# The multiply of the softmax bias moved from VectorE to ScalarE for 70 of 72 groups of an attention and soft-MoE kernel

## The chip, the cores and the metric

One Trainium2 chip, one core. The time is device microseconds of one execution; the kernel before took 293.11 us (median of 3 runs, 291.14 to 293.45). The profiled execution took 293.25 us, of which 291.5 us lie between its first and its last instruction. Engine names as in the profile: PE is TensorE, PEld its weight loads, DVE is VectorE, ACT is ScalarE, POOL is GpSimd, SP issues the transfers.

## The reference, cut to what matters

Windowed attention with a distance bias, then a soft mixture of experts over its output. The change touches the softmax of the attention alone.

```python
scores = scale * np.matmul(q, k.transpose(0, 1, 3, 2))          # (8, 8, 576, 576), scale = 1/8
mask = (rel >= 0) & (rel < window)                                # window = 128
scores = np.where(mask, scores + bias[None], -1000000000.0)
scores = scores - np.max(scores, axis=-1, keepdims=True)
attn = np.exp(scores)
attn = attn / (np.sum(attn, axis=-1, keepdims=True) + 1e-09)
attn_out = np.matmul(attn, v)
# then: logits = x @ phi; softmax over tokens and over slots; experts relu(. @ w1) @ w2; combine
```

## The kernel before, in words

Batches are 8, and a batch's 576 queries are cut into four tiles of 128 and one of 64. The unit of work is a **group**: one query tile and four of the eight heads (for the tile of 64, all eight heads), so 9 groups in a batch and 72 in all. One loop (L780 to L807) runs over the groups `i`, and in each turn it works on several groups at once, as a pipeline: the front of the softmax of group `i`, the transposes of group `i-3` (`FLAG = 3`), the product with the values of group `i-4` (`LAG = 4`), and the scores of group `i+1`. Each engine keeps the order in which the code writes its instructions (`tc.manual_schedule`), and waits at the head of its own queue.

For group `i` a turn does this:

- `softmax_front(i, i-1)` (L314): on DVE `merge` (L267, L269, L271) puts the masked halves of the 128x512 scores together in PSUM, `rowmax` (L289) takes the negated maximum of each of four heads, `inverse` (L301) takes 1/sum of group `i-1`, `bias` (L292) multiplies the negated maximum of group `i` by 1/8 into the tile `nb`, and `normalise` (L306) multiplies the four 128x128 tiles of group `i-1` by their 1/sum. `total` (L297) of group `i-1`, a copy of the four sums, runs on POOL between the exponentials that give the sums and `inverse`.
- `flip(i-3)` (L351) transposes the normalised tiles on PE into the one PSUM tile `pt`; `split(i-3)` copies it out on ACT (L358), and two masked selects on POOL (L360 and L362; L365 and L367 for the tile of 64) cut it into two triangles. The first tile of a batch needs none of the two selects.
- `run("act", i)`: on ACT `x_keep` (L417) of an earlier tile, and in five turns of a batch a small step of the token softmax (L444, L475, L479, L502, L537).
- `values(i-4)` (L387) on PE, and every second group `x_store` (L403) on ACT.
- `scores(i+1)` (L235 and L240, or L247 and L254) on PE, into the one of two PSUM tiles `s4` that group `i-1` has left.
- `expo(i)` (L341) on ACT: four exponentials of 128x128 with `nb` as their bias and with the row sums as a second output, each followed by a read of the accumulator.
- the DVE's parts of the token softmax and of the slot sums (L451 to L455, L486, L522, L533, L534) and, a piece at a time inside `softmax_front`, L543 to L546.

The call of `bias` stands in `softmax_front`, which is written ahead of `split`, `run("act", i)`, `x_store` and `expo` of the same turn. `number[key]` is a group's place from 0 to 71; `EAGER` is 2. After the loop (from about 222 us on) come the rest of the last batch, the experts and the combination; nothing there calls `bias`.

Of the kernel before, what the change touches and what calls it, by code (L numbers as in the profile page):

```python
# [28 lines left out]
SCALE = 0.125  # L29
# [13 lines left out]
EAGER = 2  # L43
# [24 lines left out]
def tile_attn_softmoe(  # L68
# [13 lines left out]
    nc = tc.nc  # L82
# [56 lines left out]
    st = {}  # L139
# [12 lines left out]
    number = {key: i for i, key in enumerate(groups)}  # L152
# [136 lines left out]
        nc.vector.tensor_reduce(st[key]["mx"][:, us], merged(key, us), axis=AX.X, op=ALU.max, negate=True)  # L289

    def bias(key, us):
        nc.vector.tensor_scalar_mul(st[key]["nb"][:, us], st[key]["mx"][:, us], SCALE)  # L292

    def total(key, us, eng=None):
        if "rs" not in st[key]:
# [18 lines left out]
    def softmax_front(new, old):  # L314
        first, eager = number[old] == 0, 0 < number[old] < EAGER
        merge(new)
        filler()
        if not eager:
            total(old, ALL, nc.gpsimd)
        if first:  # L320
            inverse(old, ALL)
            normalise(old, LO, nc.scalar.mul)
        rowmax(new, ALL)
        filler()
        if not first and not eager:
            inverse(old, ALL)
        filler()
        bias(new, ALL)
        if eager:
            total(old, ALL)  # L330
            inverse(old, ALL)
        filler()
        normalise(old, HI if first else ALL)
# [443 lines left out]
    with tc.manual_schedule(engines=ORDERED):  # L777
        scores(0)
        loads(0)
        for i in range(n):  # L780
            new = groups[i]
            run("pre", i)
            if i:
                softmax_front(new, groups[i - 1])
            else:
                for us in (LO, HI):
                    merge(new, us)
                    rowmax(new, us)
                    bias(new, us)
                    expo(new, us)  # L790
            if i >= FLAG:
                flip(groups[i - FLAG])
                split(groups[i - FLAG])
            run("act", i)
            if i >= LAG:
                values(groups[i - LAG])
                after_values(i, groups[i - LAG])
            if i + 1 < n:
                scores(i + 1)
            if i + 1 < n - 1:  # L800
                loads(i + 1)
            run("mid", i)
            if i:
                expo(new)
            run("pe", i)
            load_weights_at(i)
            run("dve", i)  # L807
# [307 lines left out]
```

## Time and profile before

| what | value |
|---|---|
| median of 3 runs | 293.11 us (291.14 to 293.45) |
| profiled execution | 293.25 us, span 291.5 us, mean granted TensorE clock 0.979 |
| PE, DVE, ACT, POOL busy | 273.9, 240.9, 206.9, 93.0 us |
| the loop over groups | first `bias` of group 1 at 9.8 us, last of group 71 at 221.9 us |
| `bias` L292 | 73 instructions: 71 of 128x4 at 156 ns, 2 of 128x2 at 169 ns |
| exponentials L341 | 288, 374 ns each, and 288 reads of 211 ns |
| copies on ACT: L358, L403, L417 | 599, 564 and 610 ns each |
| `normalise` L306 on DVE | 286, 339 ns each |
| `rowmax` L289, `merge` L269 on DVE | 698 and 686 ns each |

A row of the timeline gives start, duration, engine, line, operation, tiles, count and, in brackets, how long the engine sat idle before it and who released it. Two instructions of one engine can overlap: the next one starts before the one ahead of it has ended, so what a row costs its engine is the distance to the next start.

### The profile page before, as it was taken

The page shows a single profiled execution, that of the slowest core. Times are in us where ns is not written, and L with a number is a line of the kernel's source. Part 1 is how long each engine was busy: PE and PEld are TensorE (multiplying, and loading weights), DVE is VectorE, ACT ScalarE, POOL GpSimd, SP SyncE. Part 2 cuts the span into 40 slices and gives each one's busy share as a digit, 9 for nine tenths or more (in the row PEclk, how much of TensorE's full clock was granted, in tenths as well). Part 3 has the DMA queues.
Part 4 walks back from the last instruction along what each step waited for, and adds up shares of the span by engine and source line. Part 5 has one row for each costly group of instructions (what it writes and reads, how often), then busy time and mean ns, then how long its engine had stood idle before and what let it go on. Part 6 is the DMA issues. An engine that isn't in the chain of part 4 may idle for free.

```text
span 291.5 us, 13052 instructions
## 1 busy us (share of the span) xinstructions
PE 273.9 (94%) x5131; PEld 194.9 (67%) x5131; DVE 240.9 (83%) x746; ACT 206.9 (71%) x810; POOL 93.0 (32%) x207
## 2 busy tenths in 40 slices
PE   8499999999999999999998999999899999999990
PEld 4267777777677777776776777667677753587660
DVE  3899999999989999988999999979889455646442
ACT  2798888978988988987897887978687331035460
POOL 2025515442443344244414540644465002000000
PEclk9689999999999999999999999999999999999996
DMA  6544378877686887867686878776547779998897
GB/s 197 207 138 137 106 216 270 271 225 256 209 272 206 277 260 254 259 217 255 202 274 217 282 215 283 228 237 193 168 148 265 256 243 342 416 418 335 327 390 290
DMA packets 36753, 72.58 MB, mean 249 GB/s; under 512 B 4402, under 2 KB 15316, under 8 KB 36692
## 3 DMA queue, kind: packets, MB, share of 16 engines
q1 hardware_dynamic: 35972, 71.24, 73.4%
q8 instruction: 40, 0.66, 0.9%
q10 hardware_dynamic: 720, 0.51, 0.6%
q14 instruction: 21, 0.17, 0.2%
HBM read 62.29 MB, written 9.44 MB: 246 GB/s over the span
## 4 chain that ended last, share of the span: by engine, by line
PE 52%; DVE 38%; issue 3%; ACT 3%; POOL 2%; DVEq 0%; ACTq 0%; POOLq 0%
DVE area L306 13%; PE xp L387 10%; DVE s L289 9%; PE op L960 5%; PE s L254 5%; PE pt L351 5%; DVE s L269 5%; PE hp L924 5%; PE po L984 3%; DVE s L267 3%; PE xq L408 3%; PE s L247 2%; ACT area L341 2%; PE lp L426 2%; PE ap L509 2%
## 5 line engine op out<-in xcount | busy, mean ns | idle before, releaser
L341 ACT ACTIVATE area<-s,nb 128x128 f32<-128x128 f32 x288 | 102.5, 374 | 21.0 <-DVE nb L292 19.9
L306 DVE TENSOR_SCALAR area<-area,rs 128x128 f32<-128x128 f32 x286 | 79.4, 339 | 0.6 <-DVE nb L292 0.3
L387 PE MATMUL xp<-area 128*64 128x128 f32 (+1 forms) x1104 | 75.4, 271 | 3.5 <-POOL area L360 1.4
L387 PEld LDWEIGHTS xp<-area 128*64 128x64 f32 x1104 | 56.2, 136 | 18.9 <-issue 9.8
L341 ACT ACTIVATION_READ_ACCUMULATOR area<-s,nb 128x1 f32 x288 | 60.8, 211 | 0.0
L289 DVE TENSOR_REDUCE s<-s 128x4 f32<-128x512 f32 x71 | 49.5, 698 | 2.2
L358 ACT COPY area<-pt 128x512 f32<-128x512 f32 x70 | 41.9, 599 | 12.3 <-PE pt L351 12.0
L351 PE MATMUL pt<-unit_r,area 128*128 128x128 f32 x284 | 46.0, 285 | 0.0
L297 POOL TENSOR_SCALAR rs<-sm 128x4 f32<-128x4 f32 x70 | 13.7, 196 | 100.1 <-ACT area L341 99.2
L254 PE MATMUL s<-kq 64*32 64x160 f32 x1792 | 42.0, 302 | 0.0
L351 PEld LDWEIGHTS pt<-unit_r,area 128*128 128x128 f32 x284 | 32.2, 143 | 14.3 <-PE s L254 5.0
L360 POOL TENSOR_SCALAR_AFFINE_SELECT area<-area 128x512 f32<-128x512 f32 x48 | 31.5, 656 | 27.0 <-ACT area L358 25.9
L269 DVE COPY_PREDICATED s<-cst,s 128x512 f32<-128x512 int32 x48 | 32.9, 686 | 0.9 <-PE s L254 0.9
L362 POOL TENSOR_SCALAR_AFFINE_SELECT area<-area 128x512 f32<-128x512 f32 x48 | 31.4, 654 | 3.3
L254 PEld LDWEIGHTS s<-kq 64*32 64x32 f32 x1792 | 29.6, 108 | 0.6
L247 PE MATMUL s<-ramp,ones 64*32 64x320 bf16 x448 | 18.8, 311 | 4.8 <-ACT area L341 4.4
L403 ACT COPY area<-xp 128x512 f32<-128x512 f32 (+1 forms) x37 | 20.9, 564 | 2.2 <-PE xp L387 1.9
L408 PE MATMUL xq<-unit_r,area 128*128 128x128 f32 x136 | 22.0, 284 | 0.4
L417 ACT COPY area<-xq 128x512 f32<-128x512 f32 x34 | 20.7, 610 | 0.0
L408 PEld LDWEIGHTS xq<-unit_r,area 128*128 128x128 f32 x136 | 14.5, 141 | 6.1 <-issue 3.2
L986 ACT COPY ob<-po 128x512 f32<-128x512 f32 x19 | 10.4, 591 | 11.4 <-PE po L984 11.2
L986 DVE COPY ob<-po 128x512 f32<-128x512 f32 x17 | 11.2, 687 | 6.6 <-PE po L984 5.8
(171 smaller groups left out, 327.4 us busy)
## 6 DMA issues: line engine op xcount, KB each, us to landing
w<-w SPq DMA_DIRECT2D x53, 512.0 KB, 5.2
out<-ob SPq DMA_DIRECT2D x36, 256.0 KB, 3.2
kq<-q_t SPq DMA_DIRECT2D x69, 128.0 KB, 3.1
kq<-k_t SPq DMA_DIRECT2D x32, 256.0 KB, 4.0
area<-v_n SPq DMA_DIRECT2D x31, 256.0 KB, 4.3
area<-w SPq DMA_DIRECT2D x8, 512.0 KB, 3.9
area<-v_n SPq DMA_DIRECT2D x12, 128.0 KB, 3.2
kq<-w SPq DMA_DIRECT2D x3, 512.0 KB, 6.0
```

Source lines behind the costliest of these rows:

```text
L247: nc.tensor.matmul(s4[32 * c:32 * c + 32, 2 * par:2 * par + 2, 32 * r:32 * r + WIN], lhsT=ones[rows, 0:32], rhs=ramp[rows, h], start=True, ...
L254: nc.tensor.matmul(s4[32 * c:32 * c + 32, 2 * par + jj, 32 * r:32 * r + WIN], lhsT=qt[rows, 2 * h + jj if t == 4 else jj, 32 * r:32 * r + 32],
L269: nc.vector.copy_predicated(s4[:, :, P:2 * P], bc(mask_u, 1, 4), s4[:, :, 0:P])
L289: nc.vector.tensor_reduce(st[key]["mx"][:, us], merged(key, us), axis=AX.X, op=ALU.max, negate=True)
L306: mul(p4[:, u], p4[:, u], st[key]["rs"][:, u:u + 1])
L341: nc.scalar.activation(s["p4"][:, u], merged(key, u), AF.Exp, bias=s["nb"][:, u:u + 1], scale=SCALE, accum_out=s["sm"][:, u:u + 1],)
L351: nc.tensor.transpose(s["pt"][:, u], s["p4"][:, u], ident)
L358: copy(pa[:, us], s["pt"][:, us])
L360: nc.gpsimd.affine_select(pp[:, us], pa[:, us], [[0, m], [-1, P]], ALU.is_gt, 0.0, base=0, channel_multiplier=1)
L362: nc.gpsimd.affine_select(pa[:, us], pa[:, us], [[0, m], [1, P]], ALU.is_ge, 0.0, base=0, channel_multiplier=-1)
L387: nc.tensor.matmul(xp[D * par:D * par + D, j, 0:w], lhsT=v_slot[b, t - 1 + ph][0:rows, D * h:D * h + D], rhs=src[:, 2 * par + i] if t < 4 ...
L408: nc.tensor.transpose(xq[:, P * j:P * j + P], x_of(b, t)[:, j], ident)
```

## The change

`bias` chooses its engine by the group's number: groups 0 and 1 keep VectorE, groups 2 to 71 use ScalarE's multiply. Source and destination are the same: 128x4 from PSUM (the column of `s4` that holds the negated maximum) to `nb` in SBUF.

```diff
     def bias(key, us):
-        nc.vector.tensor_scalar_mul(st[key]["nb"][:, us], st[key]["mx"][:, us], SCALE)
+        mul = nc.vector.tensor_scalar_mul if number[key] < EAGER else nc.scalar.mul
+        mul(st[key]["nb"][:, us], st[key]["mx"][:, us], SCALE)
```

The file gets one line longer there, so that from L292 on each line of the changed kernel has a number higher by one. PE, POOL and SP have the same instructions in the same order as before.

On ACT, up to the exponentials of group 9, this stands before (`pt` is the transposed tile, `xq` and `xp` those that `x_keep` and `x_store` copy, `s` the scores, `area` the SBUF tiles):

```order
L358 COPY area<-pt 128x512
L417 COPY area<-xq 128x512
L341 ACTIVATE area,sm<-s_0_83,nb 128x128 x4
L358 COPY area<-pt 128x512
L417 COPY area<-xq 128x512
L403 COPY area<-xp 128x512
L341 ACTIVATE area,sm<-s_1_84,nb 128x128 x4
```

And this in the changed kernel:

```order
L359 COPY area<-pt 128x512
L418 COPY area<-xq 128x512
L342 ACTIVATE area,sm<-s_0_83,nb 128x128 x4
L293 ACTIVATE nb<-s_1_84 128x4
L359 COPY area<-pt 128x512
L418 COPY area<-xq 128x512
L404 COPY area<-xp 128x512
L342 ACTIVATE area,sm<-s_1_84,nb 128x128 x4
```

The multiply of a group (L293) stands behind the exponentials of the group before it and ahead of the turn's one to three copies; the group's own exponentials come behind those copies. Only for group 2, which has no copy in its turn, is it directly in front of them.

On DVE, from one group to the next (groups 4 and 5), this stands before:

```order
L269 COPY_PREDICATED s_0_83<-cst,s_0_83 128x4x128
L289 TENSOR_REDUCE s_0_83<-s_0_83 128x4
L301 RECIPROCAL rs<-rs 128x4
L292 TENSOR_SCALAR nb<-s_0_83 128x4
L306 TENSOR_SCALAR area<-area,rs 128x128 x4
L269 COPY_PREDICATED s_1_84<-cst,s_1_84 128x4x128
L289 TENSOR_REDUCE s_1_84<-s_1_84 128x4
```

And this in the changed kernel:

```order
L269 COPY_PREDICATED s_0_83<-cst,s_0_83 128x4x128
L289 TENSOR_REDUCE s_0_83<-s_0_83 128x4
L302 RECIPROCAL rs<-rs 128x4
L307 TENSOR_SCALAR area<-area,rs 128x128 x4
L269 COPY_PREDICATED s_1_84<-cst,s_1_84 128x4x128
L289 TENSOR_REDUCE s_1_84<-s_1_84 128x4
```

One instruction of each turn is gone from DVE; the others keep their order. The reciprocal of the group before (L302) now stands between the maximum and the normalisation with nothing else.

## The prediction

> **What bounds the kernel now.** I read the page first, for the loads and the chain of work that ended last.
>
> ```profile
> PE 273.9 (94%) x5131; PEld 194.9 (67%) x5131; DVE 240.9 (83%) x746; ACT 206.9 (71%) x810; POOL 93.0 (32%) x207
> PE 52%; DVE 38%; issue 3%; ACT 3%; POOL 2%; DVEq 0%; ACTq 0%; POOLq 0%
> ```
>
> ACT has the smallest share of the chain among the three large engines: it waits for others, and they seldom for it. These are averages over the whole span, so next the busy time by stretches (from the left: length, PE, PEld, DVE, ACT, POOL, clock, DMA share).
>
> ```profile
> 60.00:120.00 60.00, 59.07 (x1219) 43.53 (x1225) 57.27 (x181) 52.30 (x215) 23.92 (x53) 1.00 0.77 243
> 250.00:291.00 41.00, 34.26 (x620) 24.31 (x612) 20.09 (x41) 13.96 (x28) 0.00 (x0) 0.94 0.94 365
> ```
>
> In the loop over groups DVE is busy 95% of the time; behind it, where the change does nothing, neither DVE nor ACT is half busy. So only the loop counts. Next the groups of instructions of ACT and of DVE between 12 and 220 us (behind the bar: busy us, mean ns, us idle before them).
>
> ```profile
> L341 ACT ACTIVATE area<-s,nb 128x128 f32<-128x128 f32 x276 | 98.2, 374 | 16.8 <-DVE nb L292 15.7 <-DVE rs L297 0.4 <-POOL area L360 0.2
> L358 ACT COPY area<-pt 128x512 f32<-128x512 f32 x68 | 40.7, 599 | 12.3 <-PE pt L351 12.0
> L403 ACT COPY area<-xp 128x512 f32<-128x512 f32 (+1 forms) x37 | 20.9, 564 | 2.2 <-PE xp L387 1.9
> ```
> ```profile
> L306 DVE TENSOR_SCALAR area<-area,rs 128x128 f32<-128x128 f32 x276 | 76.8, 340 | 0.6 <-DVE nb L292 0.3
> L289 DVE TENSOR_REDUCE s<-s 128x4 f32<-128x512 f32 x68 | 47.5, 698 | 2.1
> L301 DVE RECIPROCAL rs<-rs 128x4 f32<-128x4 f32 x69 | 11.6, 168 | 0.3 <-POOL rs L297 0.3
> L292 DVE TENSOR_SCALAR nb<-s 128x4 f32<-128x4 f32 x68 | 10.6, 156 | 0.0
> L522 DVE SCALAR_TENSOR_TENSOR acc<-acc,al,ap 128x512 f32<-128x512 f32 x6 | 4.5, 746 | 4.4 <-PE ap L516 4.1 <-PE ap L509 0.3
> ```
>
> 69 reciprocals in 208 us make **3.01 us per group**. DVE idles some 10 us of it in all (these rows and small ones), about 0.15 per group: DVE sets the pace. ACT idles 31.3 us, 0.45 per group. Above all, the reciprocal hardly ever waits for the sums (0.3 us in 69): exponentials and sums of a group are long done when DVE asks for them.
>
> **The change part by part.** The pieces of one turn, from the timeline: ACT, then DVE, then POOL.
>
> ```profile
> 102.63 0.37 ACT L341 ACTIVATE area<-s,nb 128x128 f32<-128x128 f32 x1 [0.67 <-DVE nb L292]
> ...
> 110.01 0.21 ACT L341 ACTIVATION_READ_ACCUMULATOR area<-s,nb 128x1 f32 x1
> 110.10 0.60 ACT L358 COPY area<-pt 128x512 f32<-128x512 f32 x1
> 110.57 0.62 ACT L417 COPY area<-xq 128x512 f32<-128x512 f32 x1
> 111.04 0.63 ACT L403 COPY area<-xp 128x512 f32<-128x512 f32 x1
> 111.52 0.42 ACT L341 ACTIVATE area<-s,nb 128x128 f32<-128x128 f32 x1
> ...
> 112.90 0.66 ACT L358 COPY area<-pt 128x512 f32<-128x512 f32 x1
> 114.65 0.37 ACT L341 ACTIVATE area<-s,nb 128x128 f32<-128x128 f32 x1 [1.09 <-DVE nb L292]
> ```
> ```profile
> 9.01 0.18 DVE L301 RECIPROCAL rs<-rs 128x4 f32<-128x4 f32 x1 [0.62 <-POOL rs L297]
> ...
> 102.25 0.17 DVE L301 RECIPROCAL rs<-rs 128x4 f32<-128x4 f32 x1
> 102.37 0.16 DVE L292 TENSOR_SCALAR nb<-s 128x4 f32<-128x4 f32 x1
> 102.52 0.94 DVE L306 TENSOR_SCALAR area<-area,rs 128x128 f32<-128x128 f32 x4
> ```
> ```profile
> 8.78 0.19 POOL L297 TENSOR_SCALAR rs<-sm 128x4 f32<-128x4 f32 x1 [6.45 <-ACT area L341]
> ...
> 110.31 0.19 POOL L297 TENSOR_SCALAR rs<-sm 128x4 f32<-128x4 f32 x1 [1.17 <-ACT area L341]
> 110.77 0.64 POOL L360 TENSOR_SCALAR_AFFINE_SELECT area<-area 128x512 f32<-128x512 f32 x1 [0.27 <-ACT area L358]
> 111.47 0.63 POOL L362 TENSOR_SCALAR_AFFINE_SELECT area<-area 128x512 f32<-128x512 f32 x1
> ```
>
> *Removed from DVE:* 70 multiplies, each 0.15 us from its start to the next (102.37 to 102.52): 10.5 us. DVE's work per group falls from 3.01 - 0.15 idle = 2.86 to 2.71.
>
> *Added to ACT:* 70 multiplies of 128x4. The trace has none on ACT. Nearest rows:
>
> ```profile
> L213 ACT ACTIVATE tiny<-fine 128x1 f32<-128x1 f32 x1 | 0.2, 202 | 0.0
> L479 ACT ACTIVATE al<-fine,nm 128x1 f32<-128x1 f32 (+1 forms) x7 | 2.2, 318 | 0.0
> ```
>
> I take 0.20, the row of the plain one; the ends are 0.16 (DVE's own price above) and 0.32 (with a bias read per partition). The Trainium skill speaks against the move itself: "ScalarE: Activation LUTs", Rules for kernel authors, gives multiplies to VectorE. The section "What ACT_TABLE_LOAD costs" of the same page of the Trainium skill prices an ACTIVATE with constant operands at 186 ns plus 0.833 ns an element; by that, this one would take an estimated 0.19 us and the sum below would fall by 0.4 us, and no row here shows it.
>
> *Moved, and this decides:* the order of ACT's queue. Before, the copies of a turn ran while DVE still made `nb` of the group; behind 112.90 the exponentials waited 1.09 us for it, but with the copies done. Now the multiply, which must wait for `rowmax` of the same group, stands **ahead of the copies**. ACT takes its instructions in order, so the copies and with them the exponentials come only after `rowmax`. What is queued behind the waiting multiply: `split`, for which POOL's selects, the values on PE and the next transposes wait; and the exponentials, for which POOL's `total`, then DVE's reciprocal, and PE's next scores in that buffer wait.
>
> This makes a **ring over two groups**: `rowmax(i)`, multiply, copies, exponentials (i), `total(i)`, reciprocal and normalisation (i), `merge` and `rowmax` (i+2). Its pieces, by averages:
>
> - ACT: 3.01 - 0.45 = 2.56 us of work per group; plus the multiply 0.20; plus 0.10 until DVE's result reaches ACT (the multiply of 102.37 ended at 102.53, the exponential that waited for it began at 102.63); plus 0.12, by which the last accumulator read (to 110.22) outlasts the next start. Together 2.98.
> - Handoff over POOL: 110.22 to 110.31, 0.19 of work, and 0.04 to DVE (the first `total` ended at 8.97, the reciprocal that waited for it began at 9.01): 0.32.
> - DVE: 2.71, plus 0.09 by which `rowmax` outlasts the start behind it: 2.80.
>
> Sum 6.10 for two groups, 3.05 per group against 3.01. That is +2.8 us over 70 groups. DVE alone (2.71) and ACT alone (2.76) would both be faster; the ring is slower than either, because now each waits for the other.
>
> *First addition, the selects.* A normalisation that meets POOL's selects is longer:
>
> ```profile
> 96.41 0.87 DVE L306 TENSOR_SCALAR area<-area,rs 128x128 f32<-128x128 f32 x4
> ...
> 98.80 1.62 DVE L306 TENSOR_SCALAR area<-area,rs 128x128 f32<-128x128 f32 x4
> ```
> ```profile
> 98.92 0.66 POOL L360 TENSOR_SCALAR_AFFINE_SELECT area<-area 128x512 f32<-128x512 f32 x1 [0.62 <-ACT area L358]
> 99.65 0.70 POOL L362 TENSOR_SCALAR_AFFINE_SELECT area<-area 128x512 f32<-128x512 f32 x1
> ```
> ```profile
> L306 DVE TENSOR_SCALAR area<-area,rs x286: 271/280/782, 9.9 to 224.9; 128x128 f32<-128x128 f32 x143
> ```
>
> Four tiles take 0.87 with no select beside them and 1.62 with both inside; one tile takes 280 ns in the middle and 782 at most. The average is now 4 x 76.8/276 = 1.11. In the ring both meet every time: from the end of the exponentials E, the normalisation starts at E + 0.32 + 0.12 and lasts to about E + 1.3; the multiply of the next group, whose `rowmax` is done, follows E at once, `split` ends at E + 0.8, and the first select starts 0.07 later, in the middle of the normalisation, with the second behind it. So 1.62 for 1.11, in seven of nine groups (the first tile of a batch has no selects): +0.40 per ring, 6.50, **3.25 per group**.
>
> *Second addition, uneven groups.* Even and odd groups form two rings that must take turns on ACT and DVE, so the longer paces both. A turn has one to three copies (0.47 apart: 110.10, 110.57, 111.04), and the token softmax puts work on DVE in some turns only:
>
> ```profile
> 100.35 0.27 DVE L451 TENSOR_REDUCE fine<-lg 128x1 f32<-128x128 f32 x1
> ...
> 100.92 0.69 DVE L269 COPY_PREDICATED s<-cst,s 128x512 f32<-128x512 int32 x1
> ```
>
> 0.57 us here. Two rings differ thus by 0.5 to 1.0; I take 0.8, of which the slower has half over the mean: 0.4 per ring, 0.2 per group. **3.45 per group.**
>
> The sum: 3.45 - 3.01 = 0.44 us, times 70 = 30.8 us, on the profiled execution's 293.25 us (291.5 of span and 1.75 around it; the median of the runs, 293.11, is as good as the same): **324 us**. Prologue and everything behind 222 us stay and cover nothing.
>
> *What is hidden.* The later `split` delays the selects, the values and the next scores on PE:
>
> ```profile
> 88.96 0.85 PEld L387 LDWEIGHTS xp<-area 128*64 128x64 f32 x16 [0.17 <-issue]
> 89.99 0.11 PEld L247 LDWEIGHTS <-ones 64*32 64x32 bf16 x8 [0.17 <-issue]
> ```
>
> From `rowmax(i)`: 0.30 to the copy, 0.60 copy, 0.07, selects 1.34, 0.1, values 1.03 (88.96 to 89.99), scores about 0.9, `merge` and `rowmax` 1.4: 5.7 over two groups, under the 6.9 above. That way costs nothing as long as the first ring is longer.
>
> **The rivals.**
>
> 1. *DVE stays the bound.* ACT has 0.45 us idle per group for 0.20 of new work, and DVE loses 10.5 us: 282.8. It decides if the sums of group i-1 are on DVE by the time `rowmax(i)` ends, that is if the path `rowmax` to sums (2.98 + 0.32) fits into one period of 2.71. It is 0.6 too long. Chance 0.04. A queue on ACT that let copies pass a waiting multiply would end there too; the rows of ACT start in program order throughout.
> 2. *The ring without its additions*: the selects fall into other gaps, the phases settle so that long and short turns even out: 296 us. For it: before, the normalisations show 0.87 in many groups. Against it: the phases are set by E itself. Chance 0.13.
> 3. *More than I count*: the selects also hold the start of the normalisation (another 0.3 per ring), and the way over values and scores (with the batch's small tile, whose values take longer) becomes as long: 3.6 per group, 41 us more: 334. Nothing caps it in the rows. Chance 0.18.
>
> **How the numbers follow.** Forecast 0.65, rivals 0.04, 0.13, 0.18. The price of the multiply (0.16 to 0.32) enters half per group: -1.4 to +4.2 us. About 1% (3 us) can be told from no change. The range is **301 to 338**: the forecast, all of rival 3 but its far side, the upper side of rival 2. Faster 0.04 is rival 1; within 1% 0.05 is the lower part of rival 2; the rest, 0.91, is slower.
>
> **What would show it.** Right: DVE's reciprocal idles for `total` (0.3 us before) some 0.4 us or more per group; ACT's multiply waits for `rowmax` less than the exponentials waited for `nb`, or the copies no longer wait for the transposes (12 us before), since the wait stands ahead of them; DVE's busy share in the loop falls under 90%; L307 means 400 ns or more instead of 340. Wrong: a reciprocal that still finds its sums there (rival 1), an L307 at 340 (no first addition), or a period near 3.05 with DVE idle (rival 2). If PE's scores are what DVE's `merge` waits for, the ring I left hidden is the longer one.

## The result, and the profile after

The changed kernel takes **320.62 us** (median of 6 runs, 319.53 to 320.74) against 292.81 us before (6 runs): ratio 1.0942, 95% interval 1.091 to 1.0973. That is slower by 27.8 us; 324 had been predicted, in a range of 301 to 338. The profiled execution took 320.74 us with a span of 318.9 us.

The page first: loads, and the chain of work that ended last.

```profile
PE 278.7 (87%) x5131; PEld 194.7 (61%) x5131; DVE 232.3 (73%) x676; ACT 211.1 (66%) x880; POOL 99.3 (31%) x207
PE 42%; DVE 22%; ACT 16%; issue 11%; POOL 6%; DVEq 0%; POOLq 0%; ACTq 0%
```

DVE has 70 instructions less and ACT 70 more, as the order said. ACT's share of the chain went from 3 to 16%, POOL's from 2 to 6%: work that others could wait out before is now on the path. By stretches, the same one as before:

```profile
60.00:120.00 60.00, 53.66 (x1072) 38.47 (x1074) 48.28 (x143) 47.43 (x209) 23.68 (x48) 1.00 0.71 220
```

DVE fell from 95 to 80% busy, ACT from 87 to 79%, PE too. The clock is the same 1.00. No engine is the bound any more; they wait for each other. The rows of ACT and of DVE between 12 and 245 us:

```profile
L342 ACT ACTIVATE area<-s,nb 128x128 f32<-128x128 f32 x276 | 99.0, 391 | 0.1
L359 ACT COPY area<-pt 128x512 f32<-128x512 f32 x68 | 40.7, 598 | 2.3 <-PE pt L352 2.0 <-issue 0.2
L404 ACT COPY area<-xp 128x512 f32<-128x512 f32 (+1 forms) x37 | 20.7, 559 | 1.7 <-PE xp L388 1.6
...
L293 ACT ACTIVATE nb<-s 128x4 f32<-128x4 f32 x69 | 12.8, 186 | 47.6 <-DVE rs L302 39.6 <-PE xp L388 3.1 <-DVE cs L545 2.4
```
```profile
L307 DVE TENSOR_SCALAR area<-area,rs 128x128 f32<-128x128 f32 x276 | 73.2, 327 | 6.7
L289 DVE TENSOR_REDUCE s<-s 128x4 f32<-128x512 f32 x68 | 47.4, 698 | 2.1
...
L302 DVE RECIPROCAL rs<-rs 128x4 f32<-128x4 f32 x69 | 11.8, 171 | 19.6 <-POOL rs L298 19.5
...
L523 DVE SCALAR_TENSOR_TENSOR acc<-acc,al,ap 128x512 f32<-128x512 f32 x6 | 4.5, 748 | 7.1 <-PE ap L517 3.9 <-PE ap L510 3.2
```

ACT's idle time before the exponentials fell from 16.8 to 0.1 us and before the first copy from 12.3 to 2.3 us, and 47.6 us stand before the multiply: one wait, ahead of everything else in the turn. On the other side of the ring, DVE's reciprocal now waits 19.6 us for the sums (0.3 us before). DVE also waits longer for PE's slot sum (L523: 7.1 us, 4.4 before). The small copy on ACT that this sum needs now stands behind the multiply too: in one such turn the multiply starts at 117.18, the copy (L503) at 117.74, the sum on PE at 118.07, and L523 at 119.20 after 1.06 us of waiting. The prediction did not name this second way.

One turn of the ring over two groups, first ACT, then DVE, then POOL:

```profile
106.82 0.17 ACT L293 ACTIVATE nb<-s 128x4 f32<-128x4 f32 x1 [0.63 <-DVE rs L302]
106.90 0.59 ACT L359 COPY area<-pt 128x512 f32<-128x512 f32 x1
107.39 0.59 ACT L418 COPY area<-xq 128x512 f32<-128x512 f32 x1
107.86 0.38 ACT L342 ACTIVATE area<-s,nb 128x128 f32<-128x128 f32 x1
...
109.15 0.24 ACT L342 ACTIVATION_READ_ACCUMULATOR area<-s,nb 128x1 f32 x1
109.24 0.21 ACT L293 ACTIVATE nb<-s 128x4 f32<-128x4 f32 x1
109.31 0.62 ACT L359 COPY area<-pt 128x512 f32<-128x512 f32 x1
...
113.67 0.17 ACT L293 ACTIVATE nb<-s 128x4 f32<-128x4 f32 x1 [1.69 <-DVE rs L302]
```
```profile
106.03 0.70 DVE L289 TENSOR_REDUCE s<-s 128x4 f32<-128x512 f32 x1
106.64 0.17 DVE L302 RECIPROCAL rs<-rs 128x4 f32<-128x4 f32 x1
106.91 0.88 DVE L307 TENSOR_SCALAR area<-area,rs 128x128 f32<-128x128 f32 x4
...
109.69 0.18 DVE L302 RECIPROCAL rs<-rs 128x4 f32<-128x4 f32 x1 [0.55 <-POOL rs L298]
109.98 1.69 DVE L307 TENSOR_SCALAR area<-area,rs 128x128 f32<-128x128 f32 x4
...
112.88 0.70 DVE L289 TENSOR_REDUCE s<-s 128x4 f32<-128x512 f32 x1
113.49 0.17 DVE L302 RECIPROCAL rs<-rs 128x4 f32<-128x4 f32 x1
```
```profile
109.47 0.19 POOL L298 TENSOR_SCALAR rs<-sm 128x4 f32<-128x4 f32 x1 [3.00 <-ACT nb L293]
109.99 0.64 POOL L361 TENSOR_SCALAR_AFFINE_SELECT area<-area 128x512 f32<-128x512 f32 x1 [0.34 <-ACT area L359]
110.70 0.70 POOL L363 TENSOR_SCALAR_AFFINE_SELECT area<-area 128x512 f32<-128x512 f32 x1
```

The maximum of a group ends at 106.73, the multiply starts at 106.82, two copies and four exponentials follow to 109.39, POOL's `total` hands the sums over, the reciprocal starts at 109.69 after 0.55 us of waiting, the normalisation meets both selects and lasts 1.69 us, and the maximum two groups later ends at 113.58: 6.85 us for this ring over two groups. The prediction had 6.9.

A trap in reading: the rows name the reciprocal (L302) as the releaser of the multiply. It only ended last before it, at 106.81, just behind the maximum's 106.73. At 109.24 the multiply starts ahead of the reciprocal of 109.69. What it needs is the maximum.

Over the loop, from the maximum of group 2 to that of group 71 (69 steps), a group took 3.05 us before (10.99 to 221.16) and 3.40 after (11.18 to 245.74), so two groups took 6.80 on average; the difference is 24.4 us in all. The other 3 us of the span lie in the start (0.2 us), in the last turn, whose exponentials come behind its copies (1.0 us more from the start of the last maximum to them), and behind the loop (1.8 us).

### The profile page after: what moved, and what is told of

Same layout as the page of the kernel before. It is cut to its first block, busy times and chain, and to the rows that moved or that the text cites. A ratio compares the mean times of both kernels' runs of the same rounds, so it can differ in the third digit from the quotient of the medians.

```text
span 318.9 us, 13101 instructions
## 1 busy us (share of the span) xinstructions
PE 278.7 (87%) x5131; PEld 194.7 (61%) x5131; DVE 232.3 (73%) x676; ACT 211.1 (66%) x880; POOL 99.3 (31%) x207
## 4 chain that ended last, share of the span: by engine, by line
PE 42%; DVE 22%; ACT 16%; issue 11%; POOL 6%; DVEq 0%; POOLq 0%; ACTq 0%
ACT area L342 7%; PE xp L388 6%; DVE s L289 6%; PE op L961 5%; PE hp L925 4%; DVE area L307 4%; DVE s L269 4%; PE pt L352 4%; PE s L254 3%; PE po L985 3%; PE ap L510 2%; ACT area L418 2%; PE xq L409 2%; ACT area L359 2%; PE lp L427 2%
## 5 line engine op out<-in xcount | busy, mean ns | idle before, releaser
L388 PE MATMUL xp<-area 128*64 128x128 f32 (+1 forms) x1104 | 77.3, 272 | 7.3 <-ACT area L404 2.9
L307 DVE TENSOR_SCALAR area<-area,rs 128x128 f32<-128x128 f32 x286 | 75.7, 327 | 6.8
L342 ACT ACTIVATION_READ_ACCUMULATOR area<-s,nb 128x1 f32 x288 | 66.1, 229 | 0.0
L361 POOL TENSOR_SCALAR_AFFINE_SELECT area<-area 128x512 f32<-128x512 f32 x48 | 36.9, 768 | 56.5 <-ACT area L359 51.9
L293 ACT ACTIVATE nb<-s 128x4 f32<-128x4 f32 x70 | 13.0, 186 | 49.1 <-DVE rs L302 41.1
L363 POOL TENSOR_SCALAR_AFFINE_SELECT area<-area 128x512 f32<-128x512 f32 x48 | 31.4, 654 | 3.3
L302 DVE RECIPROCAL rs<-rs 128x4 f32<-128x4 f32 x72 | 12.3, 172 | 20.3 <-POOL rs L298 20.1
```

Of the source, the lines that this page charges most:

```text
L307: mul(p4[:, u], p4[:, u], st[key]["rs"][:, u:u + 1])
L342: nc.scalar.activation(s["p4"][:, u], merged(key, u), AF.Exp, bias=s["nb"][:, u:u + 1], scale=SCALE, accum_out=s["sm"][:, u:u + 1],)
L361: nc.gpsimd.affine_select(pp[:, us], pa[:, us], [[0, m], [-1, P]], ALU.is_gt, 0.0, base=0, channel_multiplier=1)
L363: nc.gpsimd.affine_select(pa[:, us], pa[:, us], [[0, m], [1, P]], ALU.is_ge, 0.0, base=0, channel_multiplier=-1)
L388: nc.tensor.matmul(xp[D * par:D * par + D, j, 0:w], lhsT=v_slot[b, t - 1 + ph][0:rows, D * h:D * h + D], rhs=src[:, 2 * par + i] if t < 4 ...
```

## The experiments

Theory O (for order): the place in ACT's queue makes the loss, through the ring. Rival E (for engine): a multiply on ACT is dear in itself. Each time stands beside that of the kernel before, run again on the same chip.

**ScalarE's multiply directly in front of the exponentials.**

```diff
-        bias(new, ALL)
+        if number[new] < EAGER:
+            bias(new, ALL)
...
             if i:
+                if i >= EAGER:
+                    bias(new, ALL)
                 expo(new)
```

> ScalarE still makes the bias of groups 2 to 71, but the multiply now stands directly in front of the exponentials, behind the copies of the turn. Theory O (the order on ScalarE does the harm): the loop is back to about 3.0 us a group, 290 to 296 us, the reciprocal of VectorE no longer waits for the sums. Rival E (a multiply on ScalarE is dear in itself, by its price and the way from VectorE to ScalarE): nearly as slow as the change, over 312 us. The removed VectorE multiply (0.15 us a group in the prediction) would give 283 us if it was worth its slot; in the profile of the change the reciprocal's start lies 0.27 us ahead of the normalisation with and without the multiply between them, by which it gives nothing.

Measured: 292.15 us against 292.27, ratio 0.9993 (0.9966 to 1.002). Same engine, same instruction, other place: the whole loss is gone, and so is the wait of DVE's reciprocal for the sums (12 to 222 us: total, times, longest):

```profile
DVE rs L302 <- POOL rs L298: 0.5, 1, 0.5
```

Theory O holds, E falls. But the time did not fall to 283 us either, which the removed DVE multiply would have given at the prediction's price. From the timeline of this kernel:

```profile
95.34 0.70 DVE L289 TENSOR_REDUCE s<-s 128x4 f32<-128x512 f32 x1
95.95 0.17 DVE L302 RECIPROCAL rs<-rs 128x4 f32<-128x4 f32 x1
96.22 0.87 DVE L307 TENSOR_SCALAR area<-area,rs 128x128 f32<-128x128 f32 x4
```

From the reciprocal's start to the normalisation's: 0.27 us, as in the kernel before, where the multiply stood between them (102.25, 102.37, 102.52 in the prediction). The normalisation needs the reciprocal's result; the multiply had filled that gap.

**An unread multiply at the change's place, VectorE's kept.**

```diff
+        if number[key] >= EAGER:
+            spare = work.tile([P, 4], F32, tag="spare", name="spare")
+            nc.scalar.mul(spare, st[key]["mx"][:, us], SCALE)
         nc.vector.tensor_scalar_mul(st[key]["nb"][:, us], st[key]["mx"][:, us], SCALE)
```

> VectorE makes the bias as before, and the exponentials read that. In addition ScalarE multiplies the same maximum at the place where the change has it, ahead of the copies, into a tile that nobody reads. Theory O: as slow as the change, 316 to 325 us, though VectorE lost nothing and the exponentials do not need ScalarE's result. Rival E, the harm comes with ScalarE's result being needed by the exponentials: under 300 us.

Measured: 323.39 us against 292.27, ratio 1.1047 (1.1012 to 1.1083). As slow as the change, though the exponentials don't use its result. But here DVE's multiply came to wait for ACT's, which reads the same maximum (12 to 245 us: total, times, longest):

```profile
DVE nb L295 <- ACT spare L294: 10.2, 41, 0.5
```

These waits of DVE sum to 10.2 us, beside a loss of 31.1 us. They can be a part of it, and this run alone doesn't settle which part.

**The same, issued behind VectorE's multiply** (the three new lines stand behind the old one).

> As the run with the unread multiply on ScalarE ahead of the copies, but issued behind VectorE's own multiply, since in that run VectorE's multiply also waited for ScalarE's (9.2 us). Here VectorE is exactly as before, and only ScalarE's queue has one more waiting instruction. Theory O: the wait ahead of the copies does it alone, 314 to 325 us. Rival: most of that run's loss came from VectorE's wait for ScalarE, 300 us or less here.

Measured: 328.72 us against 291.89, ratio 1.126 (1.1218 to 1.1302). DVE's own instructions are as before here, and it is slower still, a little past the range expected. ACT's wait is now for `nb`, which on DVE stands behind the reciprocal of the group before (12 to 245 us):

```profile
ACT spare L295 <- DVE nb L292: 44.9, 51, 2.7
L309 DVE TENSOR_SCALAR area<-area,rs 128x128 f32<-128x128 f32 x268 | 58.6, 282 | 2.7
L304 DVE RECIPROCAL rs<-rs 128x4 f32<-128x4 f32 x67 | 11.7, 175 | 30.7 <-POOL rs L300 30.3
```

This makes another ring, over a single group. One turn of it, in order of time:

```profile
110.25 0.17 ACT L295 ACTIVATE spare<-s 128x4 f32<-128x4 f32 x1 [0.65 <-DVE nb L292]
...
112.92 0.20 POOL L300 TENSOR_SCALAR rs<-sm 128x4 f32<-128x4 f32 x1 [3.04 <-ACT area L344]
113.14 0.18 DVE L304 RECIPROCAL rs<-rs 128x4 f32<-128x4 f32 x1 [0.74 <-POOL rs L300]
113.24 0.13 DVE L292 TENSOR_SCALAR nb<-s 128x4 f32<-128x4 f32 x1
113.49 0.17 ACT L295 ACTIVATE spare<-s 128x4 f32<-128x4 f32 x1 [0.65 <-DVE nb L292]
```

From multiply to multiply this is 3.24 us for one group: copies, exponentials, sums, reciprocal, `nb`, and the next multiply. Here DVE hardly ever waits for ACT's multiply (0.3 us in all), so one more waiting instruction ahead of the copies does harm even if nobody reads its result. But the 36.8 us lost here are those of this shorter way around, not of the change's ring over two groups. They also come with hardly any normalisation that meets a select (282 ns a tile).

**The same place, but a constant as the source** (`ident[:, 0:4]` for the maximum, so that nothing of VectorE is waited for).

> As the run with the unread multiply at the change's place, but it reads a constant in SBUF and so waits for nothing of VectorE. It measures the price of 70 more instructions on ScalarE alone. Theory O: 70 times 0.08 us (start to next start in the profile of the change) on an engine that idles 0.45 us a group: 292 to 295 us. Rival E (the price): 300 us or more.

Measured: 294.21 us against 292.27, ratio 1.0058 (1.0035 to 1.0081): 70 instructions cost 1.9 us in all. Their row:

```profile
L294 ACT ACTIVATE spare<-unit_r x70: 213/221/274, 11.2 to 220.1; 128x4 f32<-128x4 f32 x70
```

E falls again: the price is a fourteenth of the loss.

**No multiply at all** (the maximum goes to SBUF and is the bias, unscaled; the small constant on the row sum is 1e-30 for 1e-9).

```diff
-        bias(new, ALL)
+        if number[new] < EAGER:
+            bias(new, ALL)
...
-                bias=s["nb"][:, u:u + 1], scale=SCALE, accum_out=s["sm"][:, u:u + 1],
+                bias=s["nb" if number[key] < EAGER else "mx"][:, u:u + 1], scale=SCALE, accum_out=s["sm"][:, u:u + 1],
```

> No multiply at all for groups 2 to 71: the negated maximum is written to SBUF and the exponentials take it unscaled as their bias, which the division by the row sum takes out again (the 1e-9 on the sum becomes 1e-30). VectorE loses the multiply and ScalarE gets nothing. If VectorE's multiply was worth the 0.15 us a group of the prediction: 282 to 284 us. If it stood in a gap that the normalisation must wait out anyway, for the reciprocal's result: 290 to 294 us.

Measured: 289.01 us against 292.27, ratio 0.9881 (0.9845 to 0.9916). The scaling of the bias is left out here, and the division does not restore it: this is a measurement and not a version to use. It sizes the disputed term: 3.3 us where the prediction had 10.5. The time lies outside both ranges expected, a little under the 290 of the view that the multiply stood in a gap. The exponentials also start earlier here, so DVE's own share is 3.3 us at most.

**The multiply one place later** (behind the copy of the transposed tile, ahead of the turn's other copies).

> ScalarE's multiply stands one place later than in the change: behind the copy of the transposed tile, ahead of the other copies and steps of the turn. Theory O: the ring over two groups loses that copy, 0.47 us a ring or 0.24 a group, and the way over POOL's selects, values and scores is no longer behind the multiply: 298 to 308 us. Rival (only being directly in front of the exponentials helps, since any wait ahead of a copy stalls the queue alike): 315 us or more.

Measured: 305.63 us against 292.05, ratio 1.0461 (1.0419 to 1.0502). With one copy moved ahead of the wait, 13.6 us are lost instead of 27.8. The harm depends on what is queued behind the wait. The run moves two things at once, though: the copy itself, and with it the selects, values and scores that wait for that copy.

**The reciprocal ahead of the maximum**, with ScalarE's multiply directly in front of the exponentials, to use the 0.27 us.

```diff
+        if not first and not eager:
+            inverse(old, ALL)
         rowmax(new, ALL)
         filler()
-        if not first and not eager:
-            inverse(old, ALL)
```

> ScalarE's multiply directly in front of the exponentials, and VectorE's reciprocal of the group before moved ahead of the maximum, so that its result is there when the normalisation comes. If VectorE sets the pace and the 0.27 us from the reciprocal to the normalisation are the gap that swallowed the removed multiply: 0.15 us a group come back, 282 to 286 us. If the sums are not yet there at the earlier place, the reciprocal waits for them and holds the maximum: 290 us or more, and the reciprocal's idle time in the profile is over 5 us.

Measured: 296.2 us against 292.05, ratio 1.0133 (1.0095 to 1.0171): slower by 4 us. The gap is gone, but the sums are not there yet:

```profile
98.48 0.18 DVE L302 RECIPROCAL rs<-rs 128x4 f32<-128x4 f32 x1 [0.73 <-POOL rs L298]
98.58 0.67 DVE L289 TENSOR_REDUCE s<-s 128x4 f32<-128x512 f32 x1
99.15 0.86 DVE L307 TENSOR_SCALAR area<-area,rs 128x128 f32<-128x128 f32 x4
...
101.35 0.18 DVE L302 RECIPROCAL rs<-rs 128x4 f32<-128x4 f32 x1 [0.73 <-POOL rs L298]
```

In light turns this makes a ring over one group, 2.87 us (98.48 to 101.35). A light turn in the kernel before took 2.40, from maximum to maximum:

```profile
95.52 0.70 DVE L289 TENSOR_REDUCE s<-s 128x4 f32<-128x512 f32 x1
...
97.92 0.70 DVE L289 TENSOR_REDUCE s<-s 128x4 f32<-128x512 f32 x1
```

**The reciprocal ahead in four of nine turns only** (`number[new] % 9 in (2, 6, 7, 8)`).

> ScalarE's multiply directly in front of the exponentials, and the reciprocal ahead of the maximum only in the four turns of a batch in which it did not wait for the sums in the run that had it there in all. 0.15 us in 30 turns, 4.5 us: 287 to 290 us. If the pace of those turns is set by something else than VectorE: 291 to 294 us.

Measured: 292.37 us against 291.89, ratio 1.001 (0.9986 to 1.0033). No gain. Its normalisations mean 355 ns (338 with the multiply late and the reciprocal at its old place), and the reciprocal waits 6.4 us for the sums: what was won is given back there; which of the two decides was not tried. No version that does the whole work beat the kernel before.

**Without POOL's selects, before and after** (the masks are left out in both).

```diff
-            nc.gpsimd.affine_select(
-                pp[:, us], pa[:, us], [[0, m], [-1, P]], ALU.is_gt, 0.0, base=0, channel_multiplier=1)
-            nc.gpsimd.affine_select(
-                pa[:, us], pa[:, us], [[0, m], [1, P]], ALU.is_ge, 0.0, base=0, channel_multiplier=-1)
...
-        s.update(pd=pa, pp=pp)
+        s.update(pd=pa, pp=pa)
```

> The kernel before without POOL's two selects of each group; the masks of the triangles are left out, both products read the same copy. It is the base for the changed kernel without them. Normalisations take 0.28 us a tile instead of 0.34: 4 times 0.06 times 70 is 17 us, so 275 to 282 us; if the loop then hangs on something else, up to 288.

> The changed kernel without POOL's selects, to be set against the kernel before without them. If the first addition of the prediction holds (the change makes normalisations meet the selects more often, 14 us), the difference between the two is 10 to 17 us. If the ring alone makes the loss and the selects hit both kernels alike, the difference stays at 25 to 30 us.

Measured: 287.0 us for the kernel before so cut (it moved less than the 275 to 282 expected and stayed within the "up to 288" for a loop that hangs on something else), 305.31 us for the changed one so cut. In the first, DVE waits for PE's slot sums and scores instead (with the selects these two waits are 4.1 and 0.9 us):

```profile
DVE acc L511 <- PE ap L505: 6.0, 3, 2.1
DVE s L269 <- PE s L254: 5.6, 9, 2.5
```

The two differ by 18.3 us, with selects by 27.8: between the two views. In the second, the reciprocal waits as in the change, with no select anywhere:

```profile
DVE rs L302 <- POOL rs L298: 21.1, 32, 1.0
```

So the ring is there without selects, and with them the change costs 9.5 us more. On which way, the next two runs tell in part.

**Selects that run but are not read** (both write a tile of their own; the products read the unmasked copy, the masks are left out; the short tile's line likewise).

```diff
-                pa[:, us], pa[:, us], [[0, m], [1, P]], ALU.is_ge, 0.0, base=0, channel_multiplier=-1)
+                pp[:, us], pa[:, us], [[0, m], [1, P]], ALU.is_ge, 0.0, base=0, channel_multiplier=-1)
...
-        s.update(pd=pa, pp=pp)
+        s.update(pd=pa, pp=pa)
```

> The kernel before with POOL's selects running as ever, but into a tile that nobody reads; both products read the unmasked copy (the masks are left out). It keeps the meeting of selects and normalisations on VectorE and takes the selects off the way to the values and scores on PE. Base for the run of the changed kernel with the same edit. 288 to 293 us, since before, that way has room.

> The changed kernel with the selects unread. Without selects at all the change cost 18.3 us, with them 27.8. If the other 9.5 us are normalisations that meet selects (first addition of the prediction): the cost stays at 25 to 29 us over its base. If they are the way from the copy over the selects, the values and the next scores on PE, which the prediction called hidden: the cost falls to 17 to 21 us.

Measured: 292.26 us against 291.89 (ratio 1.0003, 0.9978 to 1.0029) for the kernel before so cut; 319.47 us (1.0928, 1.088 to 1.0975) for the changed one: 27.2 us apart. Taking the selects off the way to PE changes next to nothing, so the 9.5 us come with selects that merely run. Two ways are left. One is POOL's queue, in which `total` could stand behind a select: in the changed kernel each `total` of groups 3 to 70 starts at most 0.18 us after the last read of its sums has ended, and at most 0.15 without selects, so it is not that. What remains is the normalisation: a group's four tiles take 1.06 us on average in the changed kernel and 0.87 without selects. This is found by exclusion; no pair of runs differs in the meetings alone.

## Why the prediction was right, point by point

- **The place in the queue (right).** The multiply waits for the maximum ahead of the copies; both ends of the ring show in the rows, and moving it behind the copies takes the whole loss away (292.15 us).
- **The signs named (two of four came).** The copies hardly wait for the transposes any more (2.3 us), and DVE's busy share fell to 80%. The reciprocal idles 0.28 us a group (19.6 us in 69), less than the 0.4 named, and L307 means 327 ns, not 400.
- **What the loss consists of (right in sum; its first two terms were not measured apart).** Predicted: ring 2.8, unevenness 14, together 16.8 us; the pair without selects differs by 18.3. Predicted for the selects 14 us; measured 9.5. Sum 30.8 against 27.8. But the pair without selects is not the sum's first two terms alone: there a normalisation takes 0.87 us, while the prediction's ring has the average with selects, 1.11. How much of the 18.3 us is the ring by averages and how much the unevenness, whose 0.8 us were a choice, stays open.
- **The removed DVE multiply (wrong).** The step "DVE's work per group falls ... to 2.71" failed: the multiply stood in the 0.27 us that the normalisation must wait for the reciprocal. It was worth 3.3 us at most, not 10.5. So the ring of 6.10 us had up to 0.15 too little on DVE, which is up to 5.2 us over 70 groups.
- **The selects "meet every time" (wrong); the price of a full meeting (right).** The sign for it failed: a tile of the normalisation means 327 ns, not 400. Only 24 of the 68 groups from group 3 on wait for their sums. Those 24 normalisations take 1.32 us on average, the other 44 take 0.92 (0.88 at 106.91). A full meeting costs what was said: 1.69 us at 109.98, for the 1.62 of the prediction. An estimate from this, 24 times 0.40, gives 9.6 us, close to the 9.5 of the two pairs of runs. It fits but does not prove it: before, the selects lengthen an average normalisation more (1.11 against 0.87), and leaving them out there gains only 5.0 us (287.0 for 292.05). That a longer normalisation costs time only where the ring is tight is argued from this. The Trainium skill, "SBUF — State Buffer", Who interferes with whom, says that a VectorE multiply of this kind, when it runs in a mode that uses both of its ports, and a GpSimd instruction exclude each other for a whole instruction; the trace agrees (a tile of 0.28 us alone took 0.73 beside the select that ran from 109.99 to 110.63, and ended at 110.71).
- **ScalarE's price (too high).** 0.20 was taken; the instruction lasts 173 ns in the middle, and the next one starts 0.08 us after it (106.82 to 106.90), so the ring was given 0.12 us too much, which is 4.2 us over 70 groups. 70 of them that wait for nothing cost 1.9 us. The Trainium skill's "ScalarE: Activation LUTs", What ACT_TABLE_LOAD costs, gave an estimated 0.19, close to the duration. The same section has neighbouring ACTIVATEs overlap by about 93 ns; the trace agrees (0.17 less 0.08), and the prediction had not used that sentence.
- **The way over selects, values and scores (right).** Called hidden, and 0.6 us off with the selects unread (27.2 for 27.8).
- **Everything behind the loop (nearly).** Called unchanged; 1.8 us longer.
- **Rivals.** DVE as the bound (282.8) fell with the reciprocal's 19.6 us of waiting; the bare ring (296) and the worse case (334) lie on either side of 320.6.
- **The number (partly luck).** The removed DVE multiply made the forecast up to 5.2 us too low; ScalarE's price made it 4.2 too high and the selects 4.5. That 324 came within 3.4 us of 320.62 is owed in part to these errors cancelling.

## What to carry to other kernels

An instruction moved to an idle engine brings its wait with it: ask first where in that engine's queue it lands, and what stands behind it that did not need to wait. Sum the way from the awaited result around through every engine and back; if that takes longer than the time in which the loop now does as many groups as the way spans, no engine's idle share helps. And an instruction between a producer and its consumer on the same engine may be free: look at the distance from the producer's start to the consumer's, with and without it.

## What the runs showed of the hardware

- On DVE, a 128x4 reciprocal of 0.17 us is followed by the instruction that reads its result 0.27 us after its start; an independent 128x4 multiply between them costs no time there (102.25 to 102.52 with it, 95.95 to 96.22 without).
- On ACT, a 128x4 multiply from PSUM with a constant factor lasts 0.17 us, and a copy behind it starts 0.08 us after it; from SBUF it lasts 0.22 us.
- The normalisation's four tiles take 0.87 us alone and 1.69 with both selects running; in the trace at 109.98, two tiles that meet a select each end 0.08 us behind it (110.71 and 111.47, the selects 110.63 and 111.39).
